# Strassen's algorithm for half of an MLP up-projection, with a new order of issue

## The chip, the cores and the metric

One core of one Trainium2 chip runs the whole program. The metric is device time in microseconds of one execution; several executions are timed, and the median is given. The profile comes from one more execution, recorded by the hardware profiler; its span runs from the first to the last instruction.

## The reference

One transformer block with modulation, for 2048 tokens of width 512, all in fp32:

```
mod = (silu(c) @ w_mod)                    -> sa, ca, ga, sb, cb, gb   (512 values each)
h   = layernorm(x) * (1 + ca) + sa
x   = x + ga * attention(h)                # 32 heads of 16; linear attention:
                                           #   softmax(+-(q @ w_phi)), softmax(+-(k @ w_phi)), kv sums over all tokens
h   = layernorm(x) * (1 + cb) + sb
x   = x + gb * (gelu(layernorm(h) @ w1 + b1) @ w2 + b2)       # w1: 512 x 1376, w2: 1376 x 512
```

The up-projection is `layernorm(h) @ w1`, the down-projection the product with `w2`.

## The kernel before

**Tiling.** Tokens are worked on in 8 blocks of 256 (two tiles of 128), and for the MLP in 4 superblocks of 512 (two blocks each). Width 512 is `KC` = 4 slices of 128 partitions. The hidden width 1376 is `NFC` = 11 chunks of 128, the last one padded with repeated rows.

**fp32 by three products.** Every matmul operand is split into a rounded part (type float32r) and the remainder. `mm3` issues three matmuls, high by high, high by low, low by high, into one PSUM bank of 128x512 fp32. One up chunk of a superblock (`up`) is 4 slices x 3 = 12 matmuls of 512 columns; one chunk of the down-projection (`down`) is 4 token tiles x 3 = 12 matmuls. Splitting costs a copy with rounding on ScalarE and a subtraction on VectorE or GpSimd.

**Stages.** (1) The modulation vectors, the weights folded with `w_phi`; for blocks 0 to 7 the first LayerNorm, a transpose through DRAM, the k, v and q projections, the running kv sum in one PSUM bank (`kv_mm`). (2) The kv total is copied (`kT`), summed (`z`), transposed (`kf`); the rest of the q projections; attention of blocks 0 and 1; the splitting of w1 and w2. (3) For superblocks 0 to 3 the MLP, while the attention of the two blocks of the next superblock is prepared alongside. For one block that is: `attn_ea` (items a0, a1: maxima, exponentials, sums on VectorE, ScalarE, GpSimd; then transposes that go out to DRAM as `et_dram` and come back as `eT`), `attn_o` (o: kv times eT), `attn_w` (w: output projection), `ln_a`, `ln_b`, `ln_c` (residual and two LayerNorms), `attn_y` (y: transpose through DRAM, `yt_dram` out and `yf` back), `y_split` (yf: split into `yT` high and low). In `up` the gelu runs on ScalarE in the PSUM bank, then a rounding copy on ScalarE, the remainder on VectorE. `down` accumulates in four banks `py` until all 11 chunks are in; `mlp_out` adds `py` to the residual `x1` on VectorE and stores.

**The order.** All instructions are first collected by the class `Later`: each call is put into a queue named by program part, item and engine letter (p TensorE, a ScalarE, v VectorE, g GpSimd, s SyncE's DMA queue). The list `ISSUE` of strings, one per part, then says in which order they are issued; "+" and "-" in front of a name take from the part after or before. Matmuls issued in a row under one item go out as one group. Each engine runs its own instructions strictly in that order and waits by semaphores. `SLOTS` says, letter by letter, which buffer or PSUM bank each allocation gets: there are 8 banks and `BUFS` = 19 big buffers. All DMAs are issued from SyncE's queue. Everything recorded goes through one line of the helper, so all rows of the profile name line 218 and are told apart by tiles. The tiles' names: pg the up bank, g the gelu's result, py the down banks, pw the output projection, x1 or x the residual.

Of the kernel before, what the change touches and what calls it, by code (L numbers as in the profile page):

```python
# [47 lines left out]
    "e93cf0idhabf4g55a2h17e4i27ce25986gi96f88af4a115357h8gbbf584dec522e4g0bai8761904137ecd23b5bh77df6ae2i"  # L48
    "8507c4i322a9h829i53i9a528962i4bafe6a8h7b52ge1d00gcfggf19dgd0d2c56g9ceecc6eb0c0gc87h0g9f37i53ffb62ci7"
    "c45450fab338f8fb8c78b4374hg7h8d14263afbaab619aae55df204db9bf32fb313dd9bhe3047gagi11e",  # L50
    "bank":
    "1264710140570135353253136162435026621304533162143502472521023727652170445605353123554624602715375317"
    "153573175304761253153253215213576546037217123132712723327513246406462",
    "st6a": "01110010",
    "sta": "01010101",
    "vea": "10101001",
    "rsa": "01110110",
    "nma": "10001001",
    "dz": "001001011",
    "mxk": "1010100110011010",  # L60
    "smk": "0100011001010101",
    "rck": "0010011010101001",
    "mxq": "01011011",
    "smq": "00000000",
    "rcq": "02002110",
    "den": "10000010",
    "rd": "11010110",
    "st6b0": "10111000",
    "stb0": "01010111",
    "veb0": "01100100",  # L70
    "rsb0": "01110010",
# [12 lines left out]
    "rsc1": "01000111",
    "nmc1": "11011001",
# [3 lines left out]
-init.v -init.v -init.p db.s x0.s x1.s dk.s dq.s dm.s si.a si.v dk.s si.v bd.v si.v dk.s sr.p dq.s s0.v s0.v s0.v  # L89
s0.v s0.v s0.v s0.g sr.a dm.s s1.v s1.v s1.v n0.v s1.v n0.v dm.s s1.v s1.v n0.v s1.g fk.p dm.s ok.a x.s fq.p n0.a  # L90
ok.v fq.p oq.a n1.v n1.v m.v m.g n1.a h0.p dk.s oq.v fk.p m.v m.a n1.v ++x.s fk.p oq.a f.v ok.a oq.v fq.p n1.a ok.v
fq.p f.a m.g m.v f.v h0.p m.v pf.p n1.v m.a m.g n1.s oq.a f.v ok.a dv.s m.v m.g f.a n1.s m.a f.v pf.p n1.s m.v m.v
oq.a n1.s m.a f.v dv.s fk.p m.v ok.v f.a bg.s f.v +x.s pf.p oq.v f.v s.v f.a ok.a f.v vs.a oq.v q0.p s.v s.v s.v s.v
ok.v n1.s q1.p bg.s s.v ++s.v s.g +bg.s vs.a vs.v vs.g n.v ++s.v n.a n.v pf.p n.a n.v n.v pv1.p bg.g ++s.v k0.v n.s
h.a q0.a +s.v n.s h.a +s.v n.s q1.a +bg.g +s.v ++s.v n.s ++s.v k0.v f.a pv0.p ++++x.s h.a +bg.v f.g +bg.s h.a +s.v
+s.v k0.v f.a +bg.s +s.v ++s.v +bg.s k1.v +s.g k1.v f.g
""",
    """
pk1.p n.v -k0.v n.a n.v +s.g e.v bg.a bg.g -k0.a +bg.s +++s.v -n.s pk0.p e.v ++x.s e.g bg.a -v1.a bg.g bg.v +n.v
+n.v k1.v bg.g bg.a -k1.v q0.p +n.a -k1.v +bg.g n.a bg.v +n.a n.v +bg.g +n.v pv1.p h.a k1.v h.a e.g +n.v +bg.a n.v  # L100
++++x.s bg.a e.g ++s.v h.a n.s q1.p -k0.v e.g h.a n.s q0.a n.s f.a ++s.v +n.s f.a f.g k1.v n.s +++s.v +n.s pv0.p
q1.a k0.v f.g e.a +bg.v ++s.v -k1.a k1.v +bg.s ++s.v ++s.v -k0.v -bg.a
""",
    """
pk1.p +++s.v --k0.g --v0.a +s.v ++s.v bg.v -n.s n.s -bg.v n.s +s.g -k0.v -v1.a pv0.p --v0.v --k1.v bg.g ++s.v +n.v
--v1.v bg.v +n.a +++s.v bg.a pv1.p --bg.v bg.a +n.v bg.v -k0.v +n.a e.v -k1.a n.s h.a ++s.v --k1.v pk0.p e.g h.a
k1.v f.a ++s.v --k1.g e.v h.a +++s.v +++s.v -k0.v q1.p f.g -k1.v -k0.a h.a --v1.v k0.v -v0.a +++s.v -v0.v --v0.v
k1.v f.a k1.v -m0.p f.g -m1.p +n.v bg.p q0.p +n.v e.g bg.a q1.a k0.v +n.s +h.a +++s.v k1.v +n.s +h.a +++s.g -k1.v
+n.s e.g v1.v
""",  # L110
    """
pk1.p -k0.v -bg.s -q0.a -e.g n.s -k0.v h.a -q1.s f.a --e.v --k1.g -k0.a -bg.s ----init.v --v1.v --e.a pk0.p n.s k1.v
-bg.s f.g --v1.v --k0.v h.a -bg.s -bg.s f.a -bg.s +s.g -k0.v f.g
""",
    """
pk0.p --k0.v -k1.v -bg.s ---k0.v ---v0.v -k0.v ---k0.g n.v -k1.v pk1.p n.a -k1.v --v0.a -k0.v --k1.a --k0.g -k0.v
n.v --v0.v +n.v -k0.v n.a pv1.p --k1.v -k0.a --v1.a --k1.v +n.a k0.v --k1.g h.a k1.v --m0.p h.a --m1.p k0.v h.a
-m0.p h.a -bg.g -pv0.p n.v -k1.a --v0.v n.v f.a -k0.v n.s f.a n.s f.g -bg.a --v1.v -k0.v n.s pv0.p +n.v k1.v v1.a
n.s f.g -v1.v -v0.v +n.a k0.v k1.v -bg.g k1.v -pv1.p -k1.v n.s k0.v -bg.g +n.v k0.a +n.v
""",  # L120
    """
pk1.p -k1.a --k1.v n.s -k0.v n.s --v0.a --k0.g --v1.a n.s ----e.v h.a n.s -bg.a pk0.p ----e.s --k1.g -k1.v h.a h.a
-k0.v f.a n.s k1.v h.a -bg.g -bg.s --m1.p k0.v f.a -m0.p --v0.v -v1.v -m1.p +++lp0.s pv0.p v1.v -k1.v f.g k0.v k1.v
f.g ----e.v k1.v
""",
    """
pk1.p --k0.g h.a -k1.v -k0.v -k1.a --k1.g h.a -k1.v -v0.a pk0.p ----e.a -k0.v --bg.g f.a k1.v h.a -v0.v k1.v -k0.a
---v1.v -pv1.p k0.v h.a -k0.v f.g f.a +w1.s --bg.a -k1.v f.g -k0.v --v0.a
""",
    """  # L130
pk1.p -k1.v --k0.g ---v0.v --v1.v -k0.v -----e.v -k1.v --k1.g --m0.p -k1.a --m1.p k1.v -m0.p ---v1.v k1.v w1.s
--v1.a -pv1.p --bg.g -k0.v -----e.a -k0.v -k1.v -k0.a -k1.v pk0.p -----e.v -k1.g --v0.v -v1.v ---v0.v +a0.v -v1.v
pv0.p k0.v w1.a -k0.v -v1.a w1.g w1.a -----e.v -k0.v -m1.p k0.v m1.p w1.s w1.g pv1.p v1.v v1.v v0.v d0.s k0.v
-----e.s k0.v k1.v k0.a k1.v -k0.g d0.s v0.a k0.v -pv0.p k1.a v1.a +a0.g k0.v -v0.v k1.v k0.g q1.p -v0.a k1.v w1.a
+a0.v k1.g m0.p m2.p +a0.g m3.p d1.s kT.a +a0.g w1.s q1.a z.p +a0.a w1.g z.a kf.p q1.p z.a kf.v d1.s a0.g --bg.s
q2.p a1.g a0.v +a0.v q0.p a0.v +a0.g a1.v a1.g a0.v q2.p q2.a -v0.v a0.g a1.v a0.g q0.p a0.g a0.v a1.g a1.g a0.g
a1.g a0.g a1.v a0.v q0.a q4.p --bg.s w1.a a1.g +a0.a q1.a +a0.v t00.p a1.g q0.a t01.p t00.a q0.s t00.p +a0.v q4.a
t01.p q4.p a1.g v0.v t01.a q2.a t00.a t01.a +a0.g x0.s x1.s o00.p q2.s o01.p q1.s t10.p o00.a +a0.g t11.p o01.a
o00.v t10.p t11.a t11.p o01.v w00.p t11.a +a0.v t10.a -bg.g t10.a +a0.v o10.p la00.v o11.p +a0.g la00.a --bg.g w01.p
o10.a la00.v o11.a o10.v la00.v o11.v la00.v +a0.g la00.v +a0.g la00.g w2.s w11.p la01.v +lp1.s w1.g +a0.v la01.a  # L140
lb00.v la01.v lb00.v w10.p +a0.g la11.v la01.v lb00.v la11.a la01.v la01.v la01.g q4.a la11.v +a0.g q4.s lb01.v w1.s
q3.p la10.v lb01.v la10.a lb00.v la11.v lb01.v lb00.g la10.v la11.v lb01.v la10.v q3.p lc00.v la11.v lb01.g lc00.a
la11.g la10.v lc01.v la10.v lc01.a la10.g lb11.v +a0.g -bg.a lb10.v q3.a y0.p lb11.v y0.p y0.a lb10.v -bg.g y0.a
y0.v --bg.a y0.v
""",
    """
u0.p -lb11.v -w1.a -lb11.v -lb10.v a0.v -lb11.g u0.p a0.v -lb10.v -lc11.v a0.v a0.s -lb10.g -lc11.a -w2.g a0.s u0.p
-lc10.v a0.v -lc10.a a0.s a1.v -q3.a a0.s -y1.p a1.v a0.s -y1.p -y1.a u0.p -w1.g a0.s -y1.a -y1.v a0.s -y1.v a0.s
u1.p -q3.s ---bg.g u1.p u.a u.a a0.s u1.p u.v -w1.s u.a a1.g -w2.s u.a a0.s -w2.a a1.g d.p u.v d.p u.a a1.g u1.p u.a
a1.g d.p -w2.g a1.a d.p d.p a1.a a1.v d.p a1.g d.p a1.v d.p u.a u.v o00.p u.a a1.v o01.p -w1.a a1.g u.v u.p o01.a  # L150
+lp0.s x0.s o00.a o01.v a1.v -w2.g o00.v d.p a1.v d.p w00.p -w2.a a1.g +a0.v a1.g a1.g a1.v a1.g a1.g d.p la00.v
w01.p la00.a u.a la00.v a1.g +a0.v a1.v u.a d.p +a0.g a1.v d.p la00.v +a0.g a1.v a1.s d.p a1.v a1.s d.p +a0.g +a0.a
la00.v a1.s la01.v u.p la00.v a1.s la00.g la01.a +a0.g a1.s la01.v a1.s u.v -w2.g a1.s la01.v lb00.v d.p a1.s u.a
lb00.v d.p u.a la01.v la01.v d.p la01.g -w2.s u.p +a0.g lb01.v +a0.a a1.s u.v a1.s +a0.v x1.s -w1.g lb01.v d.p u.a
lb01.v lb00.v d.p lb01.v lb00.v +a0.v lb00.g -w2.s d.p -w2.s lb01.g d.p lc00.v -w2.g +a0.v lc00.a u.p u.a lc01.v
lc01.a u.v +a0.v -w2.a y0.v +a0.g o10.p u.a y0.v o11.p y0.s d.p o10.a y0.s o11.a o10.v d.p -w2.g y0.s o11.v w10.p
# [89 lines left out]
def adaln_hedgehog_mixer(ctx, tc, x, wqT, wkT, wv, wo, w1, w2, b2, wmodT, small_in, out):  # L246
# [714 lines left out]
    def down(b, fc):  # L961
# [3 lines left out]
        if fc == NFC - 1 - end:  # L965
            down_rows(b)
# [203 lines left out]
```

## Time and profile before

| what | value |
|---|---|
| time, median of 3 runs | 467.67 us (467.45 to 468.56) |
| span of the profiled execution | 466.6 us (no time besides the span is given for it) |
| mean granted TensorE clock | 1.000 |
| busy in the span | TensorE 458.5, VectorE 317.1, GpSimd 279.7, ScalarE 234.6 us |
| DMA | 68.05 MB, 146 GB/s over the span |

How to read it: a row of the stretches ("windows") gives, after the stretch and its length, the busy time of TensorE (PE), its weight loads (PEld), VectorE (DVE), ScalarE (ACT), GpSimd (POOL), with instruction counts, then granted clock, DMA share and GB/s. A row of the instruction groups gives engine, operation, output<-input, shapes and count, then the total busy time and the mean in ns of one, then the idle time of the engine just before them and what ended it. The chain rows give start, length and what ran. Matmuls overlap, so the mean of one (some 390 ns) is longer than the distance between two; that distance is read from the chain. A row of waits gives who waited for whom, total, times and the longest.

### The profile page before, as it was taken

To read this page: it belongs to the slowest core of one execution; us is meant where nothing else is said; L and a number is where in the kernel's file an instruction comes from. 1 tells how busy PE (TensorE), PEld (TensorE's weight loads), DVE (VectorE), ACT (ScalarE), POOL (GpSimd) and SP (SyncE) were. 2 spreads that over 40 slices of the span, in tenths; PEclk is the share of its full clock that TensorE was granted. 3 is DMA by queue.
4 is the path that set the end of the run, shared out by engine and by line. 5 is a ranking of instruction groups with operands and counts; after the bars stand their busy time and mean duration, and the time that the engine had idled before them with its cause. 6 is when DMAs were issued, how large, how long until landed. Compare 5 with 4: busy or idle time off the path is not lost.

```text
span 466.6 us, 8536 instructions
## 1 busy us (share of the span) xinstructions
PE 458.5 (98%) x3297; PEld 372.3 (80%) x3297; DVE 317.1 (68%) x612; ACT 234.6 (50%) x381; POOL 279.7 (60%) x233
## 2 busy tenths in 40 slices
PE   8999999999999999999999999999999999999996
PEld 5887888888878878978787878787788788788884
DVE  5999999989938599389797579896484472221113
ACT  4757866767440827848537743176133234422221
POOL 2369587999799998989899684756721020300000
PEclk9999999999999999999999999999999999999999
DMA  8998738492372664836837728077445504000003
GB/s 311 382 311 301 195 84 276 95 269 55 100 257 95 189 209 90 244 104 139 224 135 160 225 53 241 1 130 178 143 90 136 122 14 93 15 30 1 1 1 135
DMA packets 83673, 68.05 MB, mean 146 GB/s; under 512 B 54688, under 2 KB 70960, under 8 KB 83376
## 3 DMA queue, kind: packets, MB, share of 16 engines
q1 hardware_dynamic: 83632, 67.50, 50.9%
q8 instruction: 26, 0.43, 0.4%
q14 instruction: 15, 0.12, 0.1%
HBM read 44.94 MB, written 22.55 MB: 145 GB/s over the span
## 4 chain that ended last, share of the span: by engine, by line
PE 85%; DMA 5%; DVE 4%; POOL 2%; issue 1%; ACT 1%; SPq 0%; DVEq 0%; POOLq 0%; ACTq 0%
PE py L218 25%; PE pg L218 24%; PE pv L218 8%; PE pk L218 8%; PE pw L218 8%; PE pq L218 7%; PE pkv L218 2%; DMA wm<-in_wmodT 2%; PE po L218 1%; DVE pw L218 1%; DMA eT<-et_dram 1%; DMA wms<-in_wmodT 1%; DMA xt<-in_x 1%; PE qp L218 1%; POOL w2a L218 1%
## 5 line engine op out<-in xcount | busy, mean ns | idle before, releaser
L218 PE MATMUL pg<-yT,w 128*128 128x512 f32 (+1 forms) x528 | 115.3, 371 | 0.6 <-DVE yT L218 0.3
L218 PEld LDWEIGHTS pg<-yT,w 128*128 128x128 f32 x528 | 92.8, 188 | 18.5 <-DVE yT L218 0.5
L218 ACT ACTIVATE pg<-pg,blob 128x512 f32<-128x512 f32 x44 | 29.1, 662 | 100.6 <-PE pg L218 100.4
L218 PE MATMUL py<-w2a,g 128*128 128x512 f32 x288 | 70.7, 391 | 0.0
L218 DVE TENSOR_TENSOR g<-pg,g 128x512 fp32r<-128x512 f32 x40 | 27.2, 680 | 61.7 <-ACT g L218 61.7
L218 PEld LDWEIGHTS py<-w2a,g 128*128 128x128 f32 x288 | 53.6, 188 | 12.6 <-issue 1.6
L218 PE MATMUL pk<-wk,hT 128*128 128x512 f32 x192 | 46.2, 392 | 0.8 <-ACT hT L218 0.7
L218 PE MATMUL py<-w2b,g 128*128 128x512 f32 x192 | 46.9, 391 | 0.0
L218 PE MATMUL pv<-wvh,hT 128*128 128x512 f32 x192 | 45.9, 392 | 0.0
L218 PE MATMUL pw<-wo,oT 128*128 128x512 f32 x192 | 45.4, 390 | 0.0
L218 PE MATMUL pq<-wq,hT 128*128 128x512 f32 x192 | 45.3, 391 | 0.0
L218 PEld LDWEIGHTS pk<-wk,hT 128*128 128x128 f32 x192 | 35.6, 188 | 9.1 <-ACT hT L218 1.1
L218 PEld LDWEIGHTS py<-w2b,g 128*128 128x128 f32 x192 | 35.9, 188 | 8.1 <-issue 0.7
L218 PEld LDWEIGHTS pw<-wo,oT 128*128 128x128 f32 x192 | 35.9, 188 | 7.8 <-issue 0.4
L218 PEld LDWEIGHTS pv<-wvh,hT 128*128 128x128 f32 x192 | 35.7, 188 | 7.5
L218 PEld LDWEIGHTS pq<-wq,hT 128*128 128x128 f32 x192 | 35.8, 188 | 7.3
L218 POOL TENSOR_TENSOR ez<-eq,zb 128x1024 f32<-128x1024 f32 x15 | 36.8, 2469 | 5.5 <-ACT last L218 3.0
L218 POOL TENSOR_TENSOR yT<-yf,yT 128x256 fp32r<-128x256 f32 x24 | 17.2, 742 | 35.1 <-ACT yT L218 35.0
L218 POOL TENSOR_TENSOR ek<-ek,rck 128x1024 f32<-128x1024 f32 x16 | 30.8, 1939 | 4.5 <-DVE rck L218 2.3
L218 POOL TENSOR_TENSOR eq<-eq,rcq 128x1024 f32<-128x1024 f32 x15 | 28.9, 1937 | 0.3
L218 ACT ACTIVATE g<-pg 128x512 fp32r<-128x512 f32 x40 | 24.0, 599 | 9.5 <-PE pg L218 4.4
L218 DVE TENSOR_REDUCE smq<-eq 128x64 f32<-128x1024 f32 x16 | 19.2, 1207 | 6.8 <-ACT eq L218 6.8
(153 smaller groups left out, 783.4 us busy)
## 6 DMA issues: line engine op xcount, KB each, us to landing
et_dram<-eb SPq DMA_DIRECT2D x48, 128.0 KB, 2.9
eT<-et_dram SPq DMA_DIRECT2D x12, 512.0 KB, 5.1
xt<-in_x SPq DMA_DIRECT2D x8, 512.0 KB, 6.1
wms<-in_wmodT SPq DMA_DIRECT2D x8, 512.0 KB, 5.9
x<-in_x SPq DMA_DIRECT2D x8, 512.0 KB, 5.2
out<-x SPq DMA_DIRECT2D x15, 256.0 KB, 2.5
nt_dram<-nb SPq DMA_DIRECT2D x28, 128.0 KB, 3.4
hd<-nt_dram SPq DMA_DIRECT2D x7, 512.0 KB, 5.5
```

Of the source, the lines that this page charges most:

```text
L218: return lambda *a, **k: self.later.hold(self.letter, lambda: f(*a, **k))
```

## The change

Superblocks 2 and 3 are taken together as the two columns of a 2x2 block product: rows are the two chunks (2j, 2j+1) of a pair, the inner halves are slices 0-1 and 2-3 of the width. A full product of one pair with both superblocks is 8 half products of 6 matmuls; Strassen's algorithm in Winograd's form takes 7. The five pairs (chunks 0 to 9) are done so; chunk 10 is done as before (`ul`).

`even(j)` does chunk 2j of superblock 2 (two half products), and copies the first half product out of the bank on the way (`S1`, ScalarE). `weight_sums(j)` loads the pair's part of w1 again and forms four sums on GpSimd and splits three of them, in place over parts of the old weights (ScalarE copies, GpSimd remainders). `token_sums(h)` loads superblock 2's tokens again and forms four differences with superblock 3's (VectorE; ScalarE copies; remainders on VectorE or GpSimd), 256 tokens at a time. `odd(j)` does the other three results with five half products in two banks (items b and c): VectorE adds between half products that go into the same bank, and sets u2 and u3 aside in the constants' buffers; the three gelus are items e, f, g. Of these f has its remainder on GpSimd.

With this the down-projection of superblock 2 is split: the even chunks and chunk 10 first, whose sum is added to x1 without a store (`ev`); the odd chunks last of all, in new banks (`out2`). The residuals of blocks 4 to 7 go to DRAM and back in another row order (`xs`, `x4` to `x7`), since `y_split` no longer permutes the tokens there. `BUFS` goes from 19 to 20, `ALIGN` from 64 to 320, most small tiles get one buffer. The order of issue (`ISSUE`) and the places (`SLOTS`) are new throughout.

In the orders below only the TensorE items of three stretches and the first DMA items are picked out, and the rest is left out.

```
first DMAs, before:   db x0 x1 dk dq dm dk dk dq dm dm dm x dk
first DMAs, after:    x0 dk db x1 dk dm dk dq dm dq dm dk x dm x dv dv
kv to q, before:      m0 m2 m3 z kf q1 q2 q0         after:  m0 m2 m3 q1 kf z q2 q2
y to u, before:       q3 q3 y0 y0 u0 u0 u0 y1 y1     after:  q3 q1 y0 y0 q3 u0 u0 u0 y1 y1
superblock 1 to 2, after:   ... d o01 o00 o11 o10 d d w01 d d d w00 w10 w11 u0 u1 u4 u1 u4 u3 u2 u0 ul u3 u2 d (25 times)
the odd phase, after:       c1 c0 b1 b0 b1 b0 ul c0 c1 b0 b2 c2 b1 b2 d(7) c2 d(5) b2 d(5) b3 d(7) b3 d b4 d d c4 d
                            c3 b4 d c3 d c4 d(12) b3 b4 d ...
```

```diff
+    def half_product(o, w, t, first):
+        for k in range(2):
+            for wj, tj in ((0, 0), (0, 1), (1, 0)):
+                nc.tensor.matmul(o, w[wj][:, k], t[tj][:, k], start=first and k + wj + tj == 0, stop=k + wj == 2,
+                                 skip_group_check=True)
...
         yT = y_half(b)
+        if b >= 4:
+            for k2 in range(2):
+                src = YF[b][:, 2 * k2:2 * k2 + 2]
+                nc.scalar.activation(yT[0][k2], src, AF.Copy)
+                nc.gpsimd.tensor_sub(yT[1][k2], src, f32(yT[0][k2]))
+            return
...
+    def even(j):
+        nc.item(f"u{j}")
+        p = ps_mm("pg")
+        (a11, a12), _ = pair(j)
+        half_product(p, a11, [h[0] for h in YT[2]], True)
+        if j % 2 == 0:
+            PS["s"] = wtile("s1", [2, 512])
+        S1[j] = PS["s"][:, j % 2]
+        nc.scalar.activation(S1[j], p, AF.Copy)
+        half_product(p, a12, [h[1] for h in YT[2]], False)
+        G[2, 2 * j] = gelu(p, 2 * j)
+
+    def weight_sums(j):
+        nc.item(f"s{j}")
+        t = wtile("w1s", [KC, 2 * P])
+        nc.sync.dma_start(t, w1[:, :, 2 * j * P:2 * (j + 1) * P])
+        (a11, a12), (a21, a22) = [[t[:, 2 * k:2 * k + 2, m * P:(m + 1) * P] for k in range(2)] for m in range(2)]
+        nc.gpsimd.tensor_add(a22, a21, a22)
+        nc.gpsimd.tensor_sub(a21, a11, a21)
+        nc.gpsimd.tensor_sub(a11, a22, a11)
+        nc.gpsimd.tensor_sub(a12, a12, a11)
+        w, lo = W1[j]
+        v = w[:, :, :, 2 * j * P - lo:2 * (j + 1) * P - lo]
+        s3 = [v[:, s, 0:2, P:] for s in range(2)]
+        s24 = [v[:, s, :, :P] for s in range(2)]
+        sum1 = [SW["t"][:, s, j] for s in range(2)]
+        for dst, src in ((s3, a21), (sum1, a22), (s24, t[:, :, :P])):
+            nc.scalar.activation(dst[0], src, AF.Copy)
+            nc.gpsimd.tensor_sub(dst[1], src, f32(dst[0]))
...
+    def token_sums(h):
...
+        (b11, b21), (b12, b22), (t3, t2) = [[v[:, 0:2], v[:, 2:4]] for v in (ya, yb, z)]
+        for n, dst, p, q, lo in ((1, b11, b12, b11, nc.gpsimd), (2, t2, b22, b11, nc.vector),
+                                 (3, t3, b22, b12, nc.gpsimd), (4, b21, b21, t2, nc.vector)):
+            nc.vector.tensor_sub(dst, p, q)
+            hi, low = [v[:, :, 256 * h:256 * h + 256] for v in TS[n]]
+            nc.scalar.activation(hi, dst, AF.Copy)
+            lo.tensor_sub(low, dst, f32(hi))
+
+    def odd(j):
...
+        nc.item(f"b{j}")
+        p, c = ps_mm("pb"), ps_mm("pc")
+        half_product(p, s2, TS[2], True)
+        nc.vector.tensor_add(u2, p, S1[j])
+        half_product(p, s3, TS[3], False)
+        nc.vector.tensor_add(u3, p, S1[j])
+        half_product(p, a22, TS[4], False)
+        nc.vector.tensor_add(p, p, S1[j])
+        nc.item(f"e{j}")
+        G[2, 2 * j + 1] = gelu(p, 2 * j + 1)
+        nc.item(f"c{j}")
+        half_product(c, sum1, TS[1], True)
+        nc.vector.tensor_add(u3, c, u3)
+        half_product(c, s4, [h[1] for h in YT[3]], False)
+        nc.vector.tensor_add(c, c, u2)
+        nc.item(f"f{j}")
+        G[3, 2 * j + 1] = gelu(u3, 2 * j + 1, nc.gpsimd)
+        nc.item(f"g{j}")
+        G[3, 2 * j] = gelu(c, 2 * j)
...
+    for j in range(NJ):
+        odd(j)
+        nc.item("d")
+        for fc in (2 * j + 1, 2 * j):
+            down(3, fc, False, fc == 2 * NJ - 2)
...
+    for i in range(4):
+        py = ps_acc("py")
+        nc.item("d")
+        nc.last = None
+        for j in range(NJ):
+            down_full(py, 2, 2 * j + 1, i, j == 0, j == NJ - 1)
+        nc.item("out2")
+        add_out(2, i, py, 2 if i == 3 else 1)
```

More of the change, by code (lines that the diff above doesn't have):

```diff
@@ L200 @@
++d.p e4.a +d.p e4.a +d.p e4.v d.p
+""",
+    """
+out.v d.p out.v out.s d.p out.s d.p x7.s d.p d.p d.p d.p d.p out.v d.p out.v out.s d.p out2.v out.s d.p out2.v
+out2.s d.p out2.v out2.s d.p out2.s d.p d.p d.p out2.v out2.v out2.s out2.s
 """,
@@ L280, in adaln_hedgehog_mixer @@
     yt_dram = [dram.tile([D, 256], F32, name=f"yt_dram{b}") for b in range(NB)]
+    x1_dram = {b: dram.tile([2, 2, 2, 32, D], F32, name=f"x1_dram{b}") for b in range(4, NB)}
     nt_dram = [dram.tile([D, 256], F32, name=f"nt_dram{b}") for b in range(NB)]
@@ new lines, in odd @@
+    def odd(j):
+        sum1, s2, s3, s4, a22 = SW[j]
+        u2, u3 = [consts.tile([P, 512], F32, name="u", tag=n, bufs=1) for n in (("cb1", "gab"), ("sbb", "gbb"))[j % 2]]
+        nc.item(f"b{j}")
[17 more added lines that the diff above has]
+        G[3, 2 * j] = gelu(c, 2 * j)
@@ new lines, in adaln_hedgehog_mixer @@
+    nc.part += 1
+    SW["t"] = own("sum1", [2, NJ, 2, P], R32)
+    for b in range(4, NB):
+        nc.item(f"xs{b}")
+        nc.sync.dma_start(x1_dram[b].rearrange("i c a t d -> (c a t) i d"), X1.pop(b))
+    for j in range(NJ):
+        even(j)
+        nc.item("d")
+        down(2, 2 * j, j == 0, False)
+    nc.item("ul")
+    up(2, NFC - 1)
+    nc.item("d")
+    down(2, NFC - 1, False, True)
+    py = PY.pop(2)
+    for q in range(2):
+        x1_natural(4 + q)
+        nc.item("ev")
+        for i in range(2 * q, 2 * q + 2):
+            add_out(2, i, py[i], store=False)
@@ new lines, in adaln_hedgehog_mixer @@
+    nc.part += 1
+    for j in range(NJ):
+        weight_sums(j)
+    for h in range(2):
+        token_sums(h)
+    nc.item("ul")
+    up(3, NFC - 1)
+    nc.item("d")
+    down(3, NFC - 1, True, False)
+    for j in range(NJ):
+        odd(j)
+        nc.item("d")
+        for fc in (2 * j + 1, 2 * j):
+            down(3, fc, False, fc == 2 * NJ - 2)
+    nc.part += 1
+    py = PY.pop(3)
+    for q in range(2):
+        x1_natural(6 + q)
+        nc.item("out")
+        for i in range(2 * q, 2 * q + 2):
+            add_out(3, i, py[i])
```

376 lines of the change are left out of this document (206 added, 170 removed).

## The prediction

> **What bounds the kernel now.** I read the page first (busy time by engine), then the windows (how much of each stretch TensorE is idle), then the waits of TensorE, then the chain that ended last. The first two lines are the page, the rest the windows: in each, the busy time of TensorE, its weight loads, VectorE, ScalarE and GpSimd, then the granted clock, the DMA share and GB/s.
>
> ```profile
> span 466.6 us, 8536 instructions
> PE 458.5 (98%) x3297; PEld 372.3 (80%) x3297; DVE 317.1 (68%) x612; ACT 234.6 (50%) x381; POOL 279.7 (60%) x233
> ...
> 0.00:35.82 35.82, 33.08 (x166) 25.86 (x166) 29.58 (x87) 20.95 (x40) 15.78 (x18) 1.00 0.97 336
> 35.82:462.70 426.88, 425.45 (x3131) 346.49 (x3131) 286.80 (x524) 213.65 (x342) 263.97 (x216) 1.00 0.47 129
> 0.00:316.00 316.00, 311.82 (x2598) 254.00 (x2599) 260.09 (x510) 188.44 (x293) 251.91 (x200) 1.00 0.62 180
> 0.00:340.27 340.27, 336.09 (x2732) 273.00 (x2733) 272.48 (x528) 198.43 (x315) 269.77 (x217) 1.00 0.62 178
> 262.00:336.00 74.00, 74.00 (x409) 58.94 (x408) 57.99 (x97) 34.45 (x53) 46.26 (x47) 1.00 0.53 135
> 376.20:455.70 79.50, 79.50 (x353) 65.33 (x352) 18.73 (x33) 26.02 (x48) 7.81 (x12) 1.00 0.08 21
> ```
>
> After 35.8 us TensorE is idle for 426.88 - 425.45 = 1.4 us in 427, at clock 1.00. Before that the DMA queues set the pace (share 0.97, TensorE idle 2.7 us). The waits of TensorE name nearly all of the 1.4 us:
>
> ```profile
> PE zp L218 <- ACT kvT L218: 0.6, 1, 0.6
> PE pg L218 <- DVE yT L218: 0.3, 1, 0.3
> PE pg L218 <- ACT yT L218: 0.3, 1, 0.3
> PE po L218 <- DMA eT<-et_dram: 0.2, 1, 0.2
> ```
>
> The chain that ended last is TensorE for 85% of the span (the page's line), and from 200 us on for all of it; it closes so:
>
> ```profile
> PE 85%; DMA 5%; DVE 4%; POOL 2%; issue 1%; ACT 1%; SPq 0%; DVEq 0%; POOLq 0%; ACTq 0%
> ...
> 362.64 1.02 PE po L218 x32
> ...
> 372.05 2.04 PE py L218 x9
> 374.09 5.44 PE pg L218 x24
> ...
> 401.50 5.49 PE pg L218 x24
> ...
> 454.19 8.53 PE py L218 x35
> 462.71 0.02 issue
> 462.74 0.42 DVE x L218
> ```
>
> 24 matmuls of 512 columns in 5.44 us are 0.2267 us each: the price of a matmul here, stationary load hidden (PEld has less busy time). Span 466.6 less 462.7 leaves a tail of 3.9 us: add, store, end. So time falls when matmuls go away, if TensorE then finds its operands as promptly as now.
>
> **The change, part by part.** *Matmuls.* Up-projection of superblocks 2 and 3 is 2 x 11 chunks x 12 = 264 matmuls. After, each of five chunk pairs takes 12 (even) + 30 (odd: five half products of 6) = 42 instead of 48, and the last chunk stays 2 x 12: 234. So 30 x 0.2267 = **-6.8 us**, all on the path. The down-projection keeps its number; superblock 2's odd half moves to the very end (20 groups of three). The last adds and stores keep their form (the last tile in two halves), so the 3.9 us tail stays.
>
> *Order.* In the new order a q projection (12 matmuls, 2.7 us) stands between the last kv matmuls and the kv transpose, and another between the y transposes and the first up matmuls: these cover the waits 0.6 and 0.3 + 0.3. Between 0 and the whole 1.4 us can be had; I take **-1.2**, what those rows sum to.
>
> *First 36 us.* blob is now third on SP, the first x tile first, and one more x tile (512 KB) and more of the k and q weights precede the fourth modulation tile.
>
> ```profile
> 5.75 8.48 DMA wm<-in_wmodT
> ...
> 19.81 0.33 DVE hT L218
> 20.14 0.60 DVE wq L218
> 20.74 0.46 DVE hp L218
> 21.20 0.59 DVE st6a L218
> 21.79 0.32 DVE hT L218
> ```
>
> That tile now lands at 14.2 us, but the last hT waits for a chain on VectorE until 22, so up to some 3 us more of landing could hide if VectorE's order kept. At 336 GB/s (window row) half a MB is 1.5 us. Bounds -1.5 (VectorE's order shortened) to +1.5; I take 0, since the chain there runs through VectorE and not the load.
>
> *Added work off TensorE.* Prices for 512 columns are 0.68 us on VectorE, 0.60 on ScalarE, 1.29 on GpSimd, 0.74 there for 256:
>
> ```profile
> L218 DVE TENSOR_TENSOR g<-pg,g 128x512 fp32r<-128x512 f32 x40 | 27.2, 680 | 61.7 <-ACT g L218 61.7
> L218 ACT ACTIVATE g<-pg 128x512 fp32r<-128x512 f32 x40 | 24.0, 599 | 9.5 <-PE pg L218 4.4 <-POOL wlast L218 2.7 <-PE pw L218 1.3
> L218 POOL TENSOR_TENSOR hT<-hf,hT 128x512 fp32r<-128x512 f32 x14 | 18.0, 1294 | 2.9 <-ACT hT L218 2.9
> L218 POOL TENSOR_TENSOR yT<-yf,yT 128x256 fp32r<-128x256 f32 x24 | 17.2, 742 | 35.1 <-ACT yT L218 35.0
> ```
>
> GpSimd: weight sums 5 x (6 x 0.74 + 1.29) = 28.7, token sums 4 x 1.29 = 5.2, five gelu remainders 6.5, less 1.6 on simpler y splits: +39 us. VectorE: 25 sums 17, token sums 12 x 0.68 = 8.2, four more output adds 2.7, less the five remainders 3.4: +24.5. ScalarE: S1 copies 3.0, weight sums 5 x 1.4 (two of 256 columns at some 0.4, one of 512 at 0.6), token sums 4.8, less 1.7: +13. In the last 79.5 us (window 376 to 456) they work 18.7, 26.0 and 7.8 us now, so cost nothing there as busy time; what counts is when the operands of the odd phase are there.
>
> *PSUM handovers.* Within an odd pair the bank of b is added by VectorE after each six matmuls before the next six go in (two handovers inside the pair, one more in c): 15. If TensorE stood through each: 0.68 + some 0.15 of signalling, 12.5 us. But by the new order at least one other half product (1.36 us) or two down groups (1.36) lies between two groups on the same bank, more than 0.83. Bounds 0 and 12.5; I take 0, and **+0.7** for the place where the ul chunk's six ScalarE copies must precede the first down groups of superblock 3, one after the other.
>
> *The chain to the odd phase.* Superblock 3's tokens must be projected, normalised, transposed, differenced before its first product. Counted back from the last matmul: odd products 34.0, ul 2.7, downs 60 x 0.68 + 2 = 42.8, so c starts 79.5 us before the end, at 376.2 if the end is at 455.7. The last attention projection (w11) ends 32 us earlier (8 + 2 half products, ul, 25 down groups lie between), the o matmuls of the last token block (7) some 46 us earlier, at **330.3**; now they run at 362.6. So block 7's attention must come 32 us sooner. What prepares it:
>
> ```profile
> 272.02 3.84 POOL L218 TENSOR_TENSOR eq<-eq,rcq 128x1024 f32<-128x1024 f32 x2
> ...
> 336.43 3.83 POOL L218 TENSOR_TENSOR eq<-eq,rcq 128x1024 f32<-128x1024 f32 x2
> ...
> 397.23 4.33 POOL L218 TENSOR_TENSOR yT<-yf,yT 128x256 fp32r<-128x256 f32 x6 [10.68 <-ACT yT L218]
> ```
>
> ```profile
> 276.94 5.20 SPq L218 DMA_DIRECT2D et_dram<-eb  x8
> ...
> 283.44 1.59 SPq L218 DMA_DIRECT2D eT<-et_dram  x2
> ...
> eT<-et_dram SPq DMA_DIRECT2D x12, 512.0 KB, 5.1
> ```
>
> For block 5 the way from GpSimd's end (275.9) through the stores to landing (285.0 + 5.1) took 14.3 us. So GpSimd must end block 7 at 330.3 - 14.3 = 316; now it ends at 340.3. Of its 269.8 us up to there, eight y splits (5.9) and two bias adds (4.8) now come later, one weight sum (0.7) sooner: 259.8 us due by 316, against 251.9 done by then now. That is 8 us to win from idle GpSimd time, of which 262 to 336 alone has 74.0 - 46.3 = 27.7, mostly waits in line behind VectorE. So it fits; I take 0, bound above by nothing won: 340.3 - 5.9 - 4.8 + 0.7 + 14.3 - 330.3 = 14.3 us late.
>
> The second half: w's end at 372.05 to the last yT at 401.6 took 29.5 us, without urgency; after, differences, copy and remainder (0.68 + 0.60 + 1.29) come on top: 32.1 us against 32 of cover, were nothing faster. The new order puts LayerNorm and stores directly behind w11, so I take 0, bound +3.
>
> *DMA and SP.* x of blocks 4 to 7 goes out (4 x 512 KB) and back (16 x 128 KB), five w1 loads and two y reloads: about 7.7 MB more, at a share of 0.08 in the last window; landings of 128 to 512 KB are 2 to 6 us and issue well ahead: 0. SBUF: one more big buffer, fewer small ones; their reuse is in one engine's order: 0.
>
> **Sum.** -6.8 - 1.2 + 0 + 0.7 = -7.3, span 459.3. The page gives no time besides the span; the median of the runs lies 1.1 above it (467.67 against 466.6), so **460.4 us**.
>
> [...] The clock row reads 1.00 in every stretch above, no wait of TensorE after the start over 0.6 us. [...]
>
> **Rivals.** (1) Block 7 or the token sums late, gain partly kept: GpSimd and VectorE must pull forward work for which VectorE has 74.0 - 58.0 = 16 us idle in 262 to 336. With a third of the 14.3 us bound still missing, 4.8: 465.2. For it: GpSimd's waits there are for VectorE, so both must give. Against: only 8 of 27.7 us are needed.
> (2) The removed matmuls buy nothing, the end set by that same chain: late by 7 us, 467.5. For it: 32.1 against 32 us at the token sums; against: nothing in the old order hurried that chain.
> (3) Slower: TensorE stands at the PSUM handovers, because VectorE is busy with token sums and output adds just then. Place: the first half products, all eight banks taken (four by superblock 2's sums not yet added, four by two pairs). All 15 at 0.83 give 472.9; it turns into a loss over 7.3 / 15 = 0.5 us each. For it: VectorE's order mixes ten such sums with four output adds and a remainder at 0.68 there; against: 1.36 us of other matmuls behind each group, and VectorE at 24% in that stretch now.
>
> **How the numbers follow.** Forecast 0.64 (alone 458.0 to 463.5: all idle recovered and the start 1.5 faster, or the start 1.5 slower and a chain 2 late), rival 1 0.16, rival 2 0.08, rival 3 0.12. A change within 0.3% (1.4 us) can't be told from none. Faster is forecast and rival 1: 0.80; same rival 2: 0.08; slower 0.12. The range drops rival 3 and the bottom tenth of the first: 457.5 (-6.8 - 1.4 - 1.5, rounded down) to 467.0.
>
> **What would show it.** TensorE with 30 fewer 512-column matmuls and about 451 us busy; waits of TensorE still under 3 us in sum after the start; o of block 7 near 330 and the first sum1 product near 376; the zp and yT waits gone. Wrong if TensorE waits for po<-eT over 2 us, for the token differences, or for VectorE's u sums by several us in all, or if the start slips.

## Result and profile after

| kernel | time, median of the runs | ratio to before (95% interval) |
|---|---|---|
| before | 467.96 us (467.45 to 468.56) | |
| changed | 479.94 us (476.75 to 481.68) | 1.025 (1.0211 to 1.029) |

The change makes the kernel 12 us slower; 460.4 us was forecast. All times and ratios here and below are of undisturbed executions; one of before_shift70 that took 2623 us is left out. The profiled execution took 476.75 us, with a span of 475.0 us, 8.4 more than before. The first two lines of the page say that the 30 matmuls are gone, and that TensorE is now idle for 19 us of the span instead of 8. Helper rows are now named line 232.

```profile
span 475.0 us, 8675 instructions
...
PE 456.0 (96%) x3267; PEld 367.6 (77%) x3267; DVE 350.8 (74%) x648; ACT 241.6 (51%) x397; POOL 320.4 (67%) x269
...
q8 instruction: 25, 0.41, 0.3%
```

TensorE's waits (us in total, times, the longest) after the change:

```profile
PE pkv L232 <- issue: 10.5, 4, 3.7
PE pv L232 <- DVE wvh L232: 1.4, 1, 1.4
PE pb L232 <- DVE u L232: 1.1, 1, 1.1
PE warm L232 <- DVE ones L232: 0.9, 1, 0.9
PE scp L232 <- DVE sta L232: 0.8, 1, 0.8
```

The waits for zp and yT are gone, as forecast. In their place is a row that before does not have: 10.5 us in which TensorE waits for no other engine ("issue") in the middle of kv sums. TensorE's timeline shows the four places (start, length, what, count, idle before it and its releaser):

```profile
70.38 0.98 PE L232 MATMUL pkv<-ek,vf 128*17 128x32 f32 x95
74.12 0.44 PE L232 MATMUL pkv<-ek,vf 128*17 128x32 f32 x33 [2.77 <-issue]
...
88.32 1.59 PE L232 MATMUL pkv<-ek,vf 128*17 128x32 f32 x160
93.58 0.63 PE L232 MATMUL pkv<-ek,vf 128*17 128x32 f32 x32 [3.67 <-issue]
94.14 6.94 PE L232 MATMUL pk<-wk,hT 128*128 128x512 f32 x24
...
120.93 1.69 PE L232 MATMUL pkv<-ek,vf 128*17 128x32 f32 x177
124.64 0.31 PE L232 MATMUL pkv<-ek,vf 128*17 128x32 f32 x15 [2.02 <-issue]
...
135.99 1.86 PE L232 MATMUL pkv<-ek,vf 128*17 128x32 f32 x191
139.94 0.19 PE L232 MATMUL pkv<-ek,vf 128*17 128x32 f32 x1 [2.09 <-issue]
140.06 4.59 PE L232 MATMUL pv<-wvh,hT 128*128 128x512 f32 x12
```

A second loss stands in the rows behind two of them: 24 matmuls pk take 6.94 us, where such a row is 5.60 long elsewhere, and 12 pv 4.59 us instead of 2.88. The stretches give the reason in their clock column (third from the end, then DMA share and GB/s):

```profile
80.00:100.00 20.00, 16.33 (x250) 13.32 (x249) 13.36 (x33) 13.39 (x20) 17.76 (x11) 0.91 0.75 220
...
140.00:160.00 20.00, 20.00 (x266) 16.11 (x266) 8.94 (x8) 7.47 (x11) 16.30 (x8) 0.91 0.47 156
```

0.91 over 20 us is some 3.4 to 3.6 us at half clock; the trace's record of the clock has two spells of 3.413 us at 0.5 (from 93.3 and from 141.1 us). The 12 pv, in whose time the second spell lies, take 1.7 us longer, half of it; taken for both spells, that is 3.4 us.

**Where the 8.4 us come from.** A landmark that both kernels have is the q projection that TensorE starts once the kv total is summed and transposed. These are its rows, before and after the change:

```profile
137.63 16.61 PE L218 MATMUL pq<-wq,hT 128*128 128x512 f32 x72
```

```profile
151.19 16.63 PE L232 MATMUL pq<-wq,hT 128*128 128x512 f32 x72
```

The matmuls ahead of it are the same in both. Up to there +13.6 us: 10.5 of waits on issue and 3.4 of half clock, less the 0.6 for zp; 0.3 are left over. From there to the end of the span 323.8 instead of 329.0: -5.2. So the Strassen part gains, and the new order of the first 150 us loses more.

### The profile page after: what moved, and what is told of

Same layout as the page of the kernel before. It is cut to its first block, busy times and chain, and to the rows that moved or that the text cites. A ratio compares the mean times of both kernels' runs of the same rounds, so it can differ in the third digit from the quotient of the medians.

```text
span 475.0 us, 8675 instructions
## 1 busy us (share of the span) xinstructions
PE 456.0 (96%) x3267; PEld 367.6 (77%) x3267; DVE 350.8 (74%) x648; ACT 241.6 (51%) x397; POOL 320.4 (67%) x269
## 4 chain that ended last, share of the span: by engine, by line
PE 84%; DVE 5%; DMA 3%; issue 3%; ACT 3%; SPq 1%; DVEq 0%; ACTq 0%
PE py L232 22%; PE pg L232 14%; PE pv L232 10%; PE pw L232 9%; PE pk L232 9%; PE pq L232 9%; PE pkv L232 2%; PE pc L232 2%; PE pb L232 2%; PE po L232 2%; DMA q<-in_wqT 1%; DMA yf<-yt_dram 1%; PE fold L232 1%; SPq L232 1%; DVE tz L232 1%
## 5 line engine op out<-in xcount | busy, mean ns | idle before, releaser
L232 PE MATMUL pg<-yT,w 128*128 128x512 f32 (+1 forms) x348 | 71.4, 361 | 0.0
L232 PEld LDWEIGHTS pg<-yT,w 128*128 128x128 f32 x348 | 58.6, 189 | 10.9 <-POOL yT L232 0.8
L232 PE MATMUL pv<-wvh,hT 128*128 128x512 f32 x192 | 47.5, 402 | 1.4 <-DVE wvh L232 1.4
L232 PEld LDWEIGHTS pv<-wvh,hT 128*128 128x128 f32 x192 | 36.7, 193 | 11.9 <-issue 2.3
L232 PE MATMUL py<-w2b,g 128*128 128x512 f32 x192 | 45.8, 389 | 0.0
L232 PEld LDWEIGHTS pq<-wq,hT 128*128 128x128 f32 x192 | 35.8, 188 | 7.7 <-ACT zb L232 0.2
L232 ACT ACTIVATE pg<-pg,blob 128x512 f32<-128x512 f32 x29 | 19.3, 665 | 32.7 <-PE pg L232 29.5
L232 POOL TENSOR_TENSOR g<-u,g 128x512 fp32r<-128x512 f32 x5 | 6.5, 1294 | 33.1 <-ACT g L232 20.6
L232 POOL TENSOR_TENSOR w<-w1s,w 128x1024 fp32r<-128x1024 f32 (+2 forms) x15 | 22.5, 1505 | 2.2 <-ACT w L232 2.2
L232 PE MATMUL pb<-t,w 128*128 128x512 f32 x90 | 22.2, 391 | 1.1 <-DVE u L232 1.1
L232 DVE TENSOR_TENSOR g<-pg,g 128x512 fp32r<-128x512 f32 x25 | 16.8, 678 | 8.6 <-ACT g L232 7.1
```

The costliest lines, as they stand in the source:

```text
L232: return lambda *a, **k: self.later.hold(self.letter, lambda: f(*a, **k))
```

## Experiments

Ratios are to the kernel before, run again with each set of experiments (467.5 to 467.7 us).

**Theory A.** TensorE's instructions come in blocks of some 127 matmuls; this is read from two counts. From wait to wait lie 253, 381 and 254 matmuls in the trace, which is 2, 3 and 2 times 127 to within one, and the queue "instruction" has 25 packets in the page for 3267 matmuls, one for 131 (before: 26 for 3297, one for 127). In a kv run 127 matmuls take 1.1 us from the start of the first to the start of the last. The theory is that where two block ends fall into one such run, the block behind the second is not there yet: from the first end (127 places ahead of the wait) to the end of the wait pass 4.4, 5.0, 3.3 and 3.4 us at the four places above. In the kernel before, the four long runs of 192 have block ends at places 110, 112, 114 and 104, and the second end lies outside. By this count, whether a run has one end or two depends on how many matmuls were issued since the start. Rivals: **B**, the smaller scratch for dynamic DMA (`dynamic_dma_scratch_size=1024`), which the change also sets; **C**, the data transfers of the new order crowd out the instructions.

### Shifting the block ends

35 tiny matmul calls (70 records), shaped like those of the kv sums, at the start of the kernel before and of the changed one; in a third kernel 30 more ahead of the last tile's v projection:

```
+    for _ in range(35):
+        nc.tensor.matmul(warm[:17, :32], ones.to_broadcast([P, 17]), ones.to_broadcast([P, 32]), start=True, stop=True)
...
+        if name == "pv" and (b, i) == (NB - 1, 1):
+            for _ in range(30):
+                nc.tensor.matmul(p[:17, :32], ones.to_broadcast([P, 17]), ones.to_broadcast([P, 32]), ...)
```

> The kernel before, with 35 tiny kv-shaped fp32 matmuls (70 matmul records with their weight loads) added behind the warm-up matmuls, where TensorE is idle; their result is not used. Theory A (TensorE's instructions come in blocks of some 127 matmuls with their weight loads; where two block ends fall into one run of kv matmuls, 1.3 us apart, the second waits for a fetch): the block ends in the four long kv runs move from places 110, 112, 114 and 104 to about 40, 42, 44 and 34, so a second end comes inside each run: four new waits of TensorE for issue of 2 to 3.7 us each and one or two spells at half clock, 478 to 486 us. Theory B (the smaller scratch for dynamic DMA slows things) and theory C (data traffic at those moments delays the fetch): no change, 467 to 469 us.

> The changed kernel with the same 35 matmuls at the start. Theory A: the block ends move by 70, three of the four waits inside the kv runs go, and one new one appears in the run at 144 us (place 116 becomes 46): waits for issue 10.5 us become 2 to 4, time 466 to 472. Theories B and C: unchanged, 477 to 482.

> The changed kernel with the 35 matmuls at the start and 30 more (60 records, under 1 us of work) in front of the v projection of the last tile, into its bank before its first real matmul. Theory A: no kv run has two block ends, waits for issue under 1 us, clock 1.00 throughout, 461.5 to 465.5 us: 13 to 17 less than the changed kernel. Theories B and C: 478 to 483.

Before with 70 (before_shift70): 482.82 to 486.71 us, ratio 1.0365 (1.0321 to 1.0408). The unchanged order loses some 16 us to 35 calls that delay nothing themselves: TensorE's first row grows from 5.1 to 6.7 us, and the first kv run starts at 64.1 us as against 64.2 without them. Changed with 70 (after_shift70): 479.53 us, 1.0256 (1.0236 to 1.0276), no better than without: three waits on issue left, 5.9 us in sum, but new ones of 2.2 for po<-eT and 1.4 for pk<-ek. With 70 and 60 (after_shift70_60): 474.54 us, 1.0157 (1.0127 to 1.0187), the waits on issue down to 3.8 and the clock at 1.000.

Theory A missed the times of both shifted changed kernels, 466 to 472 and 461.5 to 465.5 us. Two things were left out. The added calls do cost time there: the first kv run starts at 71.4 and 71.7 us instead of 69.5. And a block end need not lie in the same run to matter: both profiles have a stop of 1.4 us behind 122 matmuls of a run, where the block end before lies five long matmuls ahead of the run. From there on the stops follow each other every 127 matmuls.

A profile of the first of these was taken in a run of its own:

> The kernel before with the 35 tiny matmuls at the start again, for a profile, since the profiled run of before_shift70 was disturbed (2623 us, every weight load waiting for issue). Theory A: four waits of TensorE for issue inside the kv runs, near places 167, 169, 171 and 161 of the four long runs, 8 to 14 us in all, with clock spells below 1.00 behind some.

482.34 us. TensorE's row of waits, one kv run in the timeline, and the same run in before's timeline:

```profile
PE pkv L218 <- issue: 8.7, 4, 3.1
```

```profile
81.93 1.66 PE L218 MATMUL pkv<-ek,vf 128*17 128x32 f32 x166
85.18 0.39 PE L218 MATMUL pkv<-ek,vf 128*17 128x32 f32 x26 [1.59 <-issue]
```

```profile
82.01 2.01 PE L218 MATMUL pkv<-ek,vf 128*17 128x32 f32 x192
```

For this run, the first of the four long ones, 110 - 70 + 127 = 167 is the place of the second end, and 166 matmuls stand ahead of the wait. In the other three the wait was expected at 169, 171 and 161 and stands behind 168, 170 and 161. So all four long runs break, and behind two of them the clock falls:

```profile
100.00:120.00 20.00, 16.93 (x193) 13.80 (x186) 12.09 (x26) 8.33 (x13) 12.84 (x8) 0.83 0.38 126
...
140.00:160.00 20.00, 17.44 (x255) 14.18 (x254) 8.03 (x10) 5.16 (x8) 15.87 (x9) 0.91 0.50 162
```

That is the loss of the changed kernel, in a kernel in which nothing of the change stands: the cause is the position of the matmuls.

The counter-test is a shift that leaves one end in each run: 10 calls instead of 35, ends at 90, 92, 94, 84.

> The kernel before with 10 tiny matmul calls (20 records) more at the start instead of 35 (70 records). Theory A: the block ends move from places 110, 112, 114, 104 of the four long kv runs to 90, 92, 94, 84, and the next end (127 later) still lies outside each run of 192, so no run has two ends: no wait on issue over 0.5 us, no stretch at half clock, and 467.5 to 469 us (ratio 1.000 to 1.003). Rival (the added matmuls themselves, or any shift, cost in proportion): 20/70 of the 17 us that 70 records cost, 472 to 473 us, ratio 1.010.

468.03 us, 1.0012 (1.0 to 1.0023). No wait on issue of TensorE in kv runs, no half clock. So neither added calls nor just any shift brings the loss.

### The scratch for dynamic DMA

```
-    nc = bacc.Bacc("TRN2", target_bir_lowering=False, num_devices=1)
+    nc = bacc.Bacc("TRN2", target_bir_lowering=False, num_devices=1, dynamic_dma_scratch_size=1024)
```

> The kernel before with the scratch for dynamic DMA set to 1024 as in the changed one, and nothing else. Theory A and theory C: 467 to 469 us, no wait for issue over 0.5 us. Theory B: waits for issue in the kv runs appear, 475 us or more.

467.51 us, 1.0004 (0.9995 to 1.0014): no change, B falls. C falls with the shifted kernel before, whose transfers are those of before, and by the packets of the instruction queue, which the trace records one by one: those that TensorE's stops waited for took 0.9 to 1.5 us, as long as in the kernel before.

### Splitting the kv runs in the changed kernel

Four projections are moved forward in the order, in between kv groups that stood in a row; nothing else. One of the four:

```
-... bg.s m0.p k0.v ++n.a e.g pv1.p
+... bg.s pv1.p m0.p k0.v ++n.a e.g
```

> The changed kernel with four k or v projections of 12 matmuls each moved forward by one kv group, so that no more than two groups of kv matmuls (128 records) stand in a row where there were three; nothing added or removed. Theory A (two ends of an instruction block within 1.3 us): the ends are then at least some 3.9 us apart, against the 3.2 to 4.9 us from the first end to the end of the wait that the changed kernel showed; waits of TensorE for issue fall from 10.5 to under 3 us, no half-clock spell, 461.5 to 466 us, so 13 to 17 less than the changed kernel and faster than the kernel before by 0.3 to 1.3%. Rival C (fetches are late because of data traffic at that time): the same moments, the same waits, 477 us or more. Rival D (the loss lies mostly elsewhere, as the runs with shifted ends may say: 474.5 with nearly no wait in the kv runs): 471 to 476.

after_split: 473.9 us, 1.0122 (1.0096 to 1.0148): 6 us of the 12 come back. That is the range of rival D and not that of theory A. Waits on issue 3.7 instead of 10.5. The rest moved on: 2.1 us for pk<-qs, with a spell of half clock behind it, and 1.9 for pk<-ek. The kv total is done at 149.6 and the part behind it takes 324.5. The splitting itself was incomplete, against what was said before the run: the last move only passed a kv group on to the next run, which grew from 192 matmuls to 256, and the longest wait on issue stands there.

```profile
139.75 1.83 PE L232 MATMUL pkv<-ek,vf 128*17 128x32 f32 x178
144.04 0.89 PE L232 MATMUL pkv<-ek,vf 128*17 128x32 f32 x78 [2.46 <-issue]
```

On top of it, VectorE's addition for b1 ahead of the last remainder of the token differences:

```
-... t1.a c0.p t1.a t1.g t1.v
-b1.p --yf0.g +x6.s +x6.s b0.p b1.v --yf1.g ...
+... t1.a c0.p t1.a t1.g
+b1.p --yf0.g +x6.s +x6.s b0.p b1.v t1.v --yf1.g ...
```

> The kernel of after_split with one more move: in the odd phase VectorE's addition of the first b product of pair 1 is issued ahead of a remainder of the token differences that waits for ScalarE. Theory: the wait of TensorE for the u sum (1.1 us) goes, 0.8 to 1.5 us less than after_split. Rival (VectorE is full there, the wait comes back at the next product): within 0.5 us of after_split.

split_swap: 470.36 us, 1.0056 (1.0037 to 1.0076). The wait of pb for u (1.1) is gone, and from the landmark (145.9) to the end it now takes 322.5: 2.0 less than without the swap, 6.5 less than before. That the landmark came 3.7 us earlier than in the profile above cannot come from the swap, which lies behind it; it varies between executions (see below).

The price of a matmul in the odd phase, by issuing one half product of each pair twice (30 matmuls more; the second one starts the bank anew), without the swap:

```
         half_product(c, sum1, TS[1], True)
+        half_product(c, sum1, TS[1], True)
```

> The kernel of after_split with the half product of sum1 issued twice in each odd pair (30 matmuls of 512 columns more, overwritten by the second), so that TensorE has as many matmuls as in the kernel before. If the odd phase is bound by TensorE: +6.8 us over after_split (5.5 to 7). If VectorE's additions or the token sums bind it: +0 to +3.

split_more: 475.5 us, 1.0156 (1.0131 to 1.0181). By the medians that is 1.6 more than after_split, within the range of the second answer (+0 to +3); but the part ahead of the landmark, which the edit does not touch, varies by more than that. Landmark to end 328.1, 3.6 more than after_split, 5.6 more than with the swap; 6.8 at full price. The wait for u is gone from its profile, so part of the added work ran in that time. By these single profiles the 30 saved matmuls are worth most of their price, and only when VectorE's additions are not behind the token differences.

### What is left ahead of the kv total

Four more moves. The first q projection of block 5 goes between two kv groups; VectorE's half of the value weights' remainder goes to a place ahead of GpSimd's half; five operations of key tiles go ahead of operations that had to stand (a transpose, a memset, copies behind a DMA) or were less urgent.

```
-m0.p v1.a m2.p +a0.g m3.p d1.s q1.p d0.s
+m0.p v1.a q1.p m2.p +a0.g m3.p d1.s d0.s
...
-q0.a s.v ok.a +v0.v s.v ... n.v ++x.s n.a vs.v bg.s
+q0.a s.v vs.v ok.a +v0.v s.v ... n.v ++x.s n.a bg.s
...
-... pk1.p +f.a +n.v bg.s --k1.v
+... pk1.p +f.a --k1.v +n.v bg.s
```

> The split and swapped order with four more moves: the first q projection of block 5 goes between the kv groups of tiles 13 and 14 (TensorE), VectorE's half of the value weights' low parts goes ahead of the statistics (before GpSimd's half can run), one subtraction of a key tile goes ahead of a transpose, and two subtractions and an exponential of key tiles go ahead of the work that stands. Theory A (instruction blocks): the block ends at place 52 of the run at 136.5 and place 52 of the run at 137.7 get 12 long matmuls more between them, so the wait of 2.0 us there goes to 0 to 1. VectorE and GpSimd slow each other: the operation on the value weights, 3.02 us next to GpSimd's 2.39, takes 1.21 without it, and TensorE's wait of 1.4 for it goes. The waits for the key subtractions (1.9) fall to 0.5 or less. Together 464 to 467 us, ratio 0.992 to 0.998, the kv total done at 140 to 142 us instead of 145.9. Rival (the new order is as dense as its operands allow, and each wait that goes comes back as the next one): 469 to 471, the kv total at 145 or later.

best: 465.64 us (463.87 to 468.99), 0.9959 (0.9942 to 0.9976): 0.4% faster than the kernel before, and faster than the changed one. Its page, its waits of TensorE, and the landmark in its timeline:

```profile
span 462.1 us, 8674 instructions
```

```profile
PE kvp L232 <- ACT kvT L232: 1.1, 1, 1.1
PE warm L232 <- DVE ones L232: 0.9, 1, 0.9
PE pkv L232 <- POOL ek L232: 0.9, 1, 0.9
```

```profile
139.50 16.62 PE L232 MATMUL pq<-wq,hT 128*128 128x512 f32 x72
```

No wait on issue is left, the clock is 1.000, and the landmark is 1.9 us behind that of before; behind it 322.6 us, 6.4 less than before. The value weights' rows show what VectorE and GpSimd do to each other. First the timeline of split_swap, which has the changed kernel's order there: the two run side by side. Then this kernel's, one after the other, as in the kernel before (1.21 and 2.41 us there too):

```profile
25.85 3.02 DVE L232 TENSOR_TENSOR wvh<-wv_s,wvh 128x1024 fp32r<-128x1024 f32 x1
...
25.40 2.39 POOL L232 TENSOR_TENSOR wvh<-wv_s,wvh 128x1024 fp32r<-128x1024 f32 x1 [0.37 <-ACT wvh L232]
```

```profile
22.94 1.21 DVE L232 TENSOR_TENSOR wvh<-wv_s,wvh 128x1024 fp32r<-128x1024 f32 x1
...
25.32 2.41 POOL L232 TENSOR_TENSOR wvh<-wv_s,wvh 128x1024 fp32r<-128x1024 f32 x1
```

### Why the changed kernel's executions differ

Executions of before differ by 1 to 2 us, those of the changed kernel by 5. A second profile of the changed kernel and of the last one:

> The changed kernel, unaltered, profiled a second time, to see what makes its executions differ by 5 us where those of the kernel before differ by 1. Theory A (the wait is the time to fetch the next instruction block): the waits stand at the same four places (95 of the first run, 160, 177 and 191 of the later ones) and differ in length, each 1.5 to 5 us, and half-clock stretches follow some of them or others: 476 to 482 us. Rival (the spread comes from the data transfers or from the second half): the four waits are the same to 0.3 us and the kv total ends at 151 again.

> The kernel of the last run, unaltered, profiled a second time, for the same question. Theory A: no wait on issue over 1 us in the kv runs, or one of 1 to 3 us at the run behind 88 us, whose two block ends lie 0.8 us of small matmuls and 12 long ones apart; the rest as in its first profile (462.1 us of span), 464 to 468 us. Rival: the kv total ends at 139.5 again, and the difference comes behind it.

Changed: 482.72 us, span 480.9. The four waits on issue stand at the same places and sum to 10.0 instead of 10.5, but five stretches have a lower clock instead of two:

```profile
60.00:80.00 20.00, 17.00 (x246) 13.25 (x246) 17.78 (x31) 13.38 (x29) 16.90 (x13) 0.85 0.56 160
80.00:100.00 20.00, 16.96 (x252) 13.76 (x251) 12.51 (x28) 14.18 (x21) 16.26 (x10) 0.93 0.69 198
100.00:120.00 20.00, 20.00 (x147) 16.28 (x146) 17.75 (x31) 11.59 (x16) 16.07 (x9) 0.96 0.30 105
120.00:140.00 20.00, 17.46 (x254) 14.22 (x253) 15.21 (x29) 5.30 (x7) 16.28 (x9) 0.91 0.18 70
140.00:160.00 20.00, 17.64 (x439) 14.15 (x438) 7.18 (x12) 8.30 (x13) 12.73 (x7) 0.91 0.57 187
```

The missing clock sums to 0.44; times 20 us and 2 that is 17.6 us at half clock (the clock's record: 17.1, five times 3.413), so 8.5 us lost against 3.4. That is 5.1 of the 5.9 us by which the spans differ; the landmark is at 156.9 instead of 151.2, and the part behind it takes 324.0 against 323.8. The single waits differ by 0.3 to 0.7 us (2.1, 3.0, 2.5 and 2.4 instead of 2.8, 3.7, 2.0 and 2.1), as theory A expected, but their sum hardly does; the rival (waits equal to 0.3 us, an equal landmark) was wrong. What makes these two times differ is how many spells at half clock follow the waits, two or five. The last kernel's second profile: 465.57 us, span 463.8, landmark at 141.0, 322.8 behind it, one wait on issue of 0.9 and no half clock. That wait is not at the run behind 88 us that was named but at 136.9 us, behind two block ends with 12 long matmuls between them.

## Why the prediction was wrong

*Order*, taken at -1.2, is the step that failed. The zp and yT waits it named are gone, as it said. But it costed a new order by the waits that it removes, from a list of waits of the old order, and that list cannot show what the old order avoided only by where its matmuls happened to lie. None of the prediction's signs of being wrong came: none of them looked at the stretch from 36 to 150 us, and the sum has no other term for it. Measured: +13.6 up to the kv total, of which 10.5 are shown to be block ends in kv runs (shift, counter-shift, splitting) and 3.4 the half clock behind them. The order is less dense elsewhere too, hidden by these: in after_split and split_swap 1.9 to 4 us of waits for ek and qs came up instead.

*Matmuls*, -6.8: right in number (3267 against 3297). With the forecast's -0.6 for yT and +0.7 for ul, the part behind the kv total should have gained 6.7. It gained 5.2 in the changed kernel, 6.5 once the additions for b1 were moved, 6.4 in the last kernel. TensorE's busy time fell by only 2.5 us (456.0, where about 451 was named), mostly because the 3.4 us lost at half clock count as busy (the 24 pk and 12 pv above are 1.3 and 1.7 us longer).

*Added work off TensorE.* GpSimd +40.6 (forecast 39), ScalarE +7.0 (13), VectorE +33.7 (24.5). ScalarE's is smaller mainly because it loads its activation tables 12 times instead of 16 (5.1 us less). The mis-sized term is the token differences: 12 x 0.68 = 8.2 was taken, 14.1 were needed; another 1.8 of VectorE's are the value weights. Their groups, below one whose first input lies in PSUM, in the changed kernel (total, mean of one in ns), and from its timeline one form twice, the first beside a GpSimd operation (`w<-w1s,w`, 382.12 to 383.86), the second while GpSimd stands (390.18 to 392.58):

```profile
L232 DVE TENSOR_TENSOR u<-pb,s 128x512 f32<-128x512 f32 x10 | 6.7, 683 | 9.7 <-PE pb L232 9.7
...
L232 DVE TENSOR_TENSOR t<-yr,t 128x512 fp32r<-128x512 f32 x2 | 3.1, 1549 | 0.7 <-ACT t L232 0.7
...
L232 DVE TENSOR_TENSOR yr<-yr,tz 128x512 f32<-128x512 f32 x2 | 2.5, 1234 | 0.0
L232 DVE TENSOR_TENSOR tz<-yf 128x512 f32<-128x512 f32 x2 | 2.5, 1229 | 0.0
L232 DVE TENSOR_TENSOR tz<-yf,yr 128x512 f32<-128x512 f32 x2 | 2.3, 1137 | 0.1
L232 DVE TENSOR_TENSOR yr<-yf,yr 128x512 f32<-128x512 f32 x2 | 2.0, 998 | 0.0
L232 DVE TENSOR_TENSOR t<-tz,t 128x512 fp32r<-128x512 f32 x2 | 1.7, 828 | 2.3 <-ACT t L232 2.3
```

```profile
382.64 1.77 DVE L232 TENSOR_TENSOR tz<-yf 128x512 f32<-128x512 f32 x1
...
391.16 0.69 DVE L232 TENSOR_TENSOR tz<-yf 128x512 f32<-128x512 f32 x1
```

The price 0.68 came from a row whose first input lies in PSUM (g<-pg,g), and such rows keep it here (u<-pb,s 683 ns). The row u<-pb,s did so beside GpSimd too (394.35 and 394.95 us, beside yT<-yf,yT). VectorE's twelve token differences and remainders have both inputs in SBUF: seven took 0.96 to 1.82 us with GpSimd at work beside them; two that GpSimd overlapped for less than 0.5 us took 0.67 and 0.68, and three during which it stood 0.69. For the token differences this rests on these rows; for the value weights moving the operation showed it (3.02 to 1.21 us).

*PSUM handovers*, 0: right but for one. Of 15 only one made TensorE wait, 1.1 us for u, and for the reason rival 3 named (VectorE busy with token differences), at a price of 2.0 us with its consequences. From the end of that addition (395.03 us) to TensorE's next matmul (395.17) 0.14 us passed, where some 0.15 had been taken for signalling. Rival 3's loss did not come about.

*The chain to the odd phase*, 0: right. o of block 7 starts at 340.3, 10.0 later than the 330.3 worked out, where everything ahead of it was 13.6 late; no wait for eT. The first sum1 product starts at 388.1 instead of 376.2, in the last kernel at 376.5.

*First 36 us*, 0: right in sum, 166 matmuls at 35.8 us before and 167 after, though with a new wait of 1.4 for the value weights, which the earlier start paid for. *DMA and SP*, 0: nothing in the waits speaks against it.

*The clock.* The sum has no term for a lower clock. In the changed kernel's record of it both spells at half clock are 3.413 us long, and the 12 pv around the second lost 1.7 us; the stop ahead of it was 2.1 us long. The stretches at full clock are 88.747, 44.373 and 331.093 us long, 26.0, 13.0 and 97.0 times 3.413. With the profiles cut into windows of 3.413 us along these bounds, each of the ten windows at full clock in which TensorE stood still for 1.90 to 3.37 us was followed by half clock, and none in which it stood still for 1.64 us or less. In the changed kernel's first profile two waits put 3.4 and 2.1 us into one window; the other two are cut by a window's end into 1.4 and 1.3 us, and 1.4 and 0.6, and nothing follows. In the second profile each of the four puts 1.9 to 2.5 us into one window (the first together with a wait of 0.8 us just ahead of it). So in these two profiles which waits were followed by half clock went with where the bounds of the windows fell; no run here moved a wait against them on purpose, and why the clock falls, no run shows.

## What to carry to other kernels

A list of waits prices only the order that was run: before a new order is costed, count its matmuls and look for stretches in which hundreds of tiny ones are issued in a microsecond or two, because here two ends of an instruction block within 2.5 us of each other stopped TensorE (19 of 19 cases), and 35 tiny calls more at the start brought that about in all four long kv runs of the kernel before (a ratio of 1.0365). Put long matmuls between such groups; a dozen, which brought the ends 4.0 to 4.3 us apart, helped in most places but not in all. Take the price of an operation from a row with the same places of its inputs and the same neighbour at work, not only the same shape.

## What the runs showed of the hardware

That TensorE's instructions came in blocks of some 127 matmuls with their weight loads is read from two counts. The queue "instruction" moved 25 packets for 3267 matmuls, 26 for 3297 before. Counted from a program's first matmul, all 25 waits on issue in the profiles stand behind 92 to 94 matmuls more than a multiple of 127. When two block ends came within 2.5 us of each other, TensorE stopped (19 of 19 cases) and went on 2.9 to 5.6 us after the first; at 2.9 to 4.3 us it stopped in 6 of 26, and further apart never. A single end in a run cost nothing to be seen where long matmuls filled the time before it (all long runs of before and of before_shift20).

The instruction queue's packets of 16 KB fit the loading of a block as what takes this time. In each of the 24 stops of 0.3 us or more, one had started 0.7 to 3.3 us after the first block end, took 0.9 to 1.5 us, and landed 1.1 to 1.6 us before TensorE went on. Why it started no sooner, no run shows.

A VectorE operation on 1024 columns with both inputs in SBUF took 3.02 us beside a GpSimd one of 2.39, 1.21 without it, while GpSimd's took 2.41 alone, so VectorE bore the whole cost there. In the odd phase GpSimd gave way too, but not always: six of its remainders of 512 columns took 1.50 to 1.74 us beside VectorE's differences and remainders, and three 1.29 to 1.30 (377.96, 392.58 and 395.52 us) though such an operation ran beside each for 0.7 to 1.3 us. What the two engines share that makes them slower, no run shows.
